# Dummy matmuls from a preamble constant, and tile 2's statistics placed behind tile 1's apply

## The chip, the cores and the metric

The kernel runs on one core of a Trainium2 chip. The metric is the device time of one execution in microseconds (us). The profiler's *span*, from the first to the last instruction of one execution, is 1.7 to 3.0 us shorter than the device time in the runs of these two kernels, 1.8 in the median. Engines: PE is TensorE, DVE is VectorE, ACT is ScalarE, POOL is GpSimd, SP is SyncE, which here only issues transfers.

## The reference

A layer norm of x (2048 rows of 640) feeds two branches. One is attention with 32 heads over the last 512 positions of a cache. The other is a gated feed-forward block, of whose start this study is about.

```python
xn = (x - mean(x)) / sqrt(var(x) + 1e-5)
s  = attention(xn, k_cache, v_cache, wq, wo)             # some 750 of the 920 us
g  = silu((silu(xn @ w_gate) * (xn @ w_up)) @ w_down)    # comes first
return x + s * g
```

## The kernel before

The first 13 us prepare four *tiles* of 128 rows of x, numbered 0 to 3. For each tile DVE makes the statistics in two halves and aggregates them, ACT takes the square root of the variance (Sqrt), DVE takes the reciprocal and applies it to x ("apply"), TensorE transposes the result by five matmuls against an identity matrix, and ACT copies the two parts out to `xnT`. The feed-forward matmuls of that tile follow. Before any of this, dummy matmuls on a zeroed tile keep TensorE busy, which is meant to have its clock at full rate when real work comes.

```python
zero_t = ffw.tile([P, 512], bf, name="zero_t")
nc.vector.memset(zero_t[:], 0.0)
...
load_x(0, (nc.scalar, nc.sync))
load_x(1, (nc.scalar,))
load_first(slice(0, 2), (nc.sync, nc.scalar))  # chunks 0, 1 of the gate and up weights
load_first(slice(2, NC))                       # chunks 2, 3, 4: gate, then up, both on SyncE
load_x(2, (nc.scalar,))
...
load_x(3)
...
keep_warm(9)        # nine dummy matmuls of 512 columns on zero_t
keep_warm(6, P)     # six of 128

def ln_stats(t, between=None):
    ...
    for g in range(ng):                 # two halves of the 640 columns
        nc.vector.bn_stats(stats[:, g, :], x_t[t][:, ...])
        if g == 0 and between:
            between()                   # apply of another tile stands between them
    nc.vector.bn_aggr(ln[b][0][:, ti, :], stats[:])

def ready(t):
    ...                                 # five transposes into tps[0], tps[1]
    for tp, cs in zip(tps, PARTS):
        if cs.stop == NC and 1 <= t < 3:
            ln_sqrt(t + 1)              # Sqrt of the next tile between the two copies
        ... nc.scalar.copy(xnT[:, cs, rows], part)

for t in range(4):
    ...
    for k, (f, s, cs) in enumerate(order):
        if k == len(order) * 7 // 10 and t < 3:
            if t < 2:
                ln_stats(t + 2, lambda: ln_apply(t + 1))
            else:
                ln_apply(t + 1)
            ready(t + 1)
            ...
        hidden_mm(first[f][s][:, rows], s, f, rows, cs)
```

For tile 0, `order` has 30 matmuls: twelve on weight chunks 0 and 1, nine on gate chunks 2 to 4, then (after tile 1's transposes) nine on up chunks 2 to 4. The second load of gate weights ("the late gate weights" below: 288 KB, chunks 2 to 4) is thus wanted just before tile 1's transposes.

The softmax here doesn't subtract the row's maximum and nothing guards it: scores larger than these inputs give would overflow.

## Time and profile before

| | before |
|---|---|
| median of the first 3 runs | 920.73 us (920.32 to 921.08) |
| profiled span | 919.1 us |
| TensorE busy | 912.6 us (99%) |
| tile 1's / 2's / 3's transposes start | 8.54 / 10.50 / 12.45 us |
| last group of matmuls starts | 915.06 us |

A line of the timeline gives start, duration, engine, source line, operation, output<-input, shape and count; in brackets stands the idle time of the engine before it and what ended that. A line of the waits gives who waited for whom, the total, the number and the longest.

### The profile page before, as it was taken

To read this page: it belongs to the slowest core of one execution; us is meant where nothing else is said; L and a number is where in the kernel's file an instruction comes from. 1 tells how busy PE (TensorE), PEld (TensorE's weight loads), DVE (VectorE), ACT (ScalarE), POOL (GpSimd) and SP (SyncE) were. 2 spreads that over 40 slices of the span, in tenths; PEclk is the share of its full clock that TensorE was granted. 3 is DMA by queue.
4 is the path that set the end of the run, shared out by engine and by line. 5 is a ranking of instruction groups with operands and counts; after the bars stand their busy time and mean duration, and the time that the engine had idled before them with its cause. 6 is when DMAs were issued, how large, how long until landed. Compare 5 with 4: busy or idle time off the path is not lost.

```text
span 919.1 us, 23152 instructions
## 1 busy us (share of the span) xinstructions
PE 912.6 (99%) x9898; PEld 548.9 (60%) x9920; DVE 601.7 (65%) x844; ACT 474.4 (52%) x840; POOL 85.3 (9%) x269
## 2 busy tenths in 40 slices
PE   9999999999999999999999999999999999999998
PEld 6444444465757575656565656666666666665665
DVE  6443321467777777777777777676867777777657
ACT  4222222556464656565656565655555555556471
POOL 0000000000000000000000000000000000001976
PEclk9999999999999999999999999999999999999999
DMA  9412430045352544263534343435243444343526
GB/s 302 76 34 65 90 84 1 1 75 113 54 113 49 112 51 107 54 109 54 109 58 109 57 109 52 109 54 107 56 85 76 88 79 78 87 71 102 118 61 166
DMA packets 248166, 77.53 MB, mean 84 GB/s; under 512 B 228992, under 2 KB 248064, under 8 KB 248064
## 3 DMA queue, kind: packets, MB, share of 16 engines
q1 hardware_dynamic: 245696, 73.39, 39.5%
q10 hardware_dynamic: 2368, 2.67, 0.9%
q8 instruction: 77, 1.26, 0.6%
q14 instruction: 25, 0.20, 0.1%
HBM read 38.93 MB, written 2.62 MB: 45 GB/s over the span
## 4 chain that ended last, share of the span: by engine, by line
PE 99%; DMA 1%; DVE 0%; ACTq 0%; issue 0%
PE mm L448 22%; PE sc L462 18%; PE mm L487 16%; PE sc L602 15%; PE sc L282 11%; PE mm L312 6%; PE sc L572 4%; PE sc L564 2%; PE mm L539 2%; PE mm L564 1%; DMA x_t<-in_A_x_dram 1%; PE gu L282 0%; PE mm L321 0%; PE sc L539 0%; PE sc L487 0%
## 5 line engine op out<-in xcount | busy, mean ns | idle before, releaser
L466 ACT ACTIVATE p_t<-sc 128x1024 bf16<-128x1024 f32 x254 | 253.0, 1023 | 120.3 <-PE sc L462 120.3
L453 DVE TENSOR_REDUCE qT<-mm 128x512 bf16<-128x1024 f32 x189 | 231.2, 1223 | 99.0 <-PE mm L448 96.5
L517 ACT ACTIVATE O_b<-mm,r 128x192 bf16<-128x192 f32 x486 | 165.0, 422 | 183.1 <-issue 136.6
L448 PE MATMUL mm<-xnT,wq_p 64*128 64x512 bf16 x1890 | 237.5, 376 | 0.0
L462 PE MATMUL sc<-qT,khat 64*128 64x512 bf16 x1524 | 198.0, 376 | 0.0
L487 PEld LDWEIGHTS <-p_t 64*128 64x128 bf16 x3584 | 159.0, 94 | 33.8
L487 PE MATMUL mm<-V_p,p_t 64*128 64x193 bf16 x3520 | 176.4, 243 | 0.0
L615 DVE TENSOR_TENSOR s_m<-s_m,sc 128x1024 f32<-128x1024 f32 x108 | 131.9, 1221 | 60.7 <-PE sc L602 52.3
L602 PE MATMUL sc<-wo_p,OT_b 64*128 64x512 bf16 x1296 | 168.9, 376 | 0.0
L448 PEld LDWEIGHTS <-wq_p 64*128 64x128 bf16 x1890 | 105.0, 94 | 98.9 <-issue 0.8
L462 PEld LDWEIGHTS <-khat 64*128 64x128 bf16 x1536 | 85.3, 94 | 80.4 <-DVE s_t L615 0.3
L602 PEld LDWEIGHTS <-OT_b 64*128 64x128 bf16 x1296 | 70.3, 94 | 44.1 <-issue 0.3
L615 DVE TENSOR_TENSOR s_t<-s_t,sc 128x512 f32<-128x512 f32 x108 | 74.2, 687 | 28.4 <-PE sc L572 26.6
L589 POOL MEMSET turn_t<- 128x1 f32 x220 | 21.6, 98 | 700.0 <-PE mm L487 506.0
L290 DVE TENSOR_TENSOR hT<-sc,sg 128x512 bf16<-128x512 f32 x46 | 31.7, 692 | 81.5 <-ACT sg L289 81.5
L289 ACT ACTIVATE sg<-sc 128x512 bf16<-128x512 f32 x46 | 27.3, 596 | 69.8 <-PE sc L282 66.7
L282 PE MATMUL sc<-xnT,wg_sb 128*128 128x512 bf16 (+1 forms) x255 | 60.1, 354 | 0.5
L282 PE MATMUL sc<-xnT,wu_sb 128*128 128x512 bf16 (+1 forms) x255 | 59.5, 355 | 0.2
L572 PE MATMUL sc<-OT_b,wo_p 64*128 64x512 bf16 (+1 forms) x345 | 50.3, 376 | 0.0
L312 PE MATMUL mm<-wd_sb,hT 128*128 128x512 bf16 x189 | 43.6, 379 | 0.2
L282 PEld LDWEIGHTS <-wu_sb 128*128 128x128 bf16 x285 | 27.1, 98 | 26.8 <-issue 0.3
L282 PEld LDWEIGHTS <-wg_sb 128*128 128x128 bf16 x285 | 27.2, 98 | 26.3
(83 smaller groups left out, 418.3 us busy)
## 6 DMA issues: line engine op xcount, KB each, us to landing
wo_p<-in_A_wo_dram SPq DMA_DIRECT2D x16, 480.0 KB, 4.7
K_p<-in_A_k_cache_dram SPq DMA_DIRECT2D x32, 192.0 KB, 4.4
V_p<-in_A_v_cache_dram SPq DMA_DIRECT2D x32, 192.0 KB, 3.3
wq_p<-in_A_wq_dram SPq DMA_DIRECT2D x64, 80.0 KB, 2.8
wq_p<-in_A_wq_dram SPq DMA_DIRECT2D x16, 160.0 KB, 3.0
x_t<-in_A_x_dram SPq DMA_DIRECT2D x13, 160.0 KB, 3.0
x_b<-in_A_x_dram SPq DMA_DIRECT2D x4, 512.0 KB, 6.1
OT_b<-O_b SPq DMA_TRANSPOSE x124, 2.8
```

What stands on the lines that cost most here:

```text
L282: nc.tensor.matmul(out, w_sb[:, c, f * P : (f + 1) * P], xnT[:, c, qc], start=(c == 0), stop=(c == NC - 1),)
L290: nc.vector.tensor_tensor(hTs[b][:, f, :], u, sg[:], ALU.mult)
L312: nc.tensor.matmul(dn, at, by, start=(f == 0), stop=(f == NF - 1))
L448: nc.tensor.matmul(q_ps[:, h, :], pairs[pr]["wq"][r, c, j * P : (j + 1) * P], xnT[r, c, b * 512 : (b + 1) * 512], start=(c == 0), stop=(c ...
L453: nc.vector.reduce_sum(qTs[i][:, j, :], q_ps[:, :, :].rearrange("p h n -> p n h"), axis=AX.X)
L462: nc.tensor.matmul(sc[:, h, :], khat[r, j, ks], qT[r, j, :], start=(j == 0), stop=(j == 2))
L466: nc.scalar.activation(p_t[:, :, :], sc[:, :, :], ACT.Exp, scale=scale)
L487: m = nc.tensor.matmul(acc[:, k, h * 256 : h * 256 + Dh + 1], Ps[i][kc][r, h, qt * P : (qt + 1) * P], V_p[r, kc, h, 0 : Dh + 1], start=(p ...
L517: nc.scalar.activation(O_b[:, qt, h, :], a_k[:, h, 0:Dh], ACT.Copy, scale=r[:, k, h, :])
L572: nc.tensor.matmul(ps.rearrange("p (t q) -> p t q", q=P), pairs[i // NB]["wo"][r, j, MC:D], OTs[i][:, :, :].rearrange("p (t j) q -> p j t ...
L602: m = nc.tensor.matmul(ps[:, k, :], OTs[i][r, 3 * (2 * half + k) + j, :], pairs[i // NB]["wo"][r, j, MAIN], start=(turn == 0 and j == 0), ...
L615: nc.vector.tensor_tensor(to, to, ps, ALU.add)
```

## The change

Its intent is to take two waits off TensorE at the start. The dummy matmuls read a constant that GpSimd writes before the engines start, so they need no memset by DVE. Tile 1's apply no longer stands between the halves of tile 2's statistics, whose data may not have landed; those statistics and tile 2's Sqrt come after tile 1's apply, transposes and copies. The diff, whole but for line numbers:

```diff
-        zero_t = ffw.tile([P, 512], bf, name="zero_t")
-        nc.vector.memset(zero_t[:], 0.0)
...
         def keep_warm(n, cols=512):
+            ones = [nc.const_aps.tensor(1.0, (P, k), bf) for k in (P, cols)]
             for _ in range(n):
-                nc.tensor.matmul(
-                    first[2][1][:, 0:cols], zero_t[:, 0:P], zero_t[:, 0:cols], start=True, stop=True
-                )
-
-        keep_warm(9)
+                nc.tensor.matmul(first[2][1][:, 0:cols], *ones, start=True, stop=True)
+
+        keep_warm(10)
         keep_warm(6, P)
...
-                if cs.stop == NC and 1 <= t < 3:
-                    ln_sqrt(t + 1)
+                if cs.stop == NC and t == 2:
+                    ln_sqrt(3)
...
-                    if t < 2:
-                        ln_stats(t + 2, lambda: ln_apply(t + 1))
+                    if t == 1:
+                        ln_stats(3, lambda: ln_apply(2))
                     else:
                         ln_apply(t + 1)
                     ready(t + 1)
-                    if t == 2:
+                    if t == 0:
+                        ln_stats(2)
+                        ln_sqrt(2)
+                    elif t == 2:
                         nc.scalar.activation(act_t[:], one_t[:], ACT.Silu)
```

## The prediction

> **What bounds the kernel now.** I read the page first, then the waits of TensorE over the whole span, then the timeline of the first 13 us engine by engine, because the diff touches only that stretch. The page says who owns the span: the matmul engine is busy from end to end, and the chain that ended last is nearly all its own instructions.
>
> ```profile
> span 919.1 us, 23152 instructions
> PE 912.6 (99%) x9898; PEld 548.9 (60%) x9920; DVE 601.7 (65%) x844; ACT 474.4 (52%) x840; POOL 85.3 (9%) x269
> PE 99%; DMA 1%; DVE 0%; ACTq 0%; issue 0%
> ```
>
> The reader is to see 919.1 - 912.6 = 6.5 us in which TensorE is not busy, and a DMA share of 1% of the chain: nothing else can be won by moving VectorE or ScalarE work. The view of TensorE's waits shows only two waits with a releaser in the whole run, both in the stretch that the diff touches:
>
> ```profile
> PE gu L230 <- DVE zero_t L176: 1.2, 1, 1.2
> PE tp L335 <- DVE xn L267: 0.5, 1, 0.5
> ```
>
> The first is the start (dummy matmuls wait for the zeroed tile), the second is the transposes of x tile 1 waiting for that tile's apply. So at most these 1.2 + 0.5 us are in play. VectorE's timeline gives the reason for the second:
>
> ```profile
> 6.27 0.21 DVE L246 BATCH_NORM_AGGREGATE mv<-stats 128x2 f32<-128x12 f32 x1
> 7.44 0.49 DVE L243 BATCH_NORM_STATS2 stats<-x_t 128x6 f32<-128x320 bf16 x1 [0.97 <-DMA x_t<-in_A_x_dram]
> 7.85 0.14 DVE L265 RECIPROCAL rstd<-rstd 128x1 f32<-128x1 f32 x1
> 8.03 0.45 DVE L267 TENSOR_SCALAR xn<-x_t,mv,rstd 128x640 bf16<-128x640 bf16 x1
> 8.39 0.48 DVE L243 BATCH_NORM_STATS2 stats<-x_t 128x6 f32<-128x320 bf16 x1
> 8.91 0.21 DVE L246 BATCH_NORM_AGGREGATE mv<-stats 128x2 f32<-128x12 f32 x1
> 9.04 0.44 DVE L243 BATCH_NORM_STATS2 stats<-x_t 128x6 f32<-128x320 bf16 x1
> ```
>
> At 7.44 VectorE takes the first half of tile 2's statistics, for which it idled 0.97 us until x tile 2 landed. Tile 1's reciprocal and apply stand behind it, though their input was there earlier, as ScalarE's timeline shows:
>
> ```profile
> 6.84 0.30 ACT L256 ACTIVATE rstd<-mv,eps_t 128x1 f32<-128x1 f32 x1
> 8.86 0.37 ACT L343 COPY xnT<-tp 128x256 bf16<-128x256 bf16 x1 [1.72 <-PE tp L335]
> 9.16 0.29 ACT L256 ACTIVATE rstd<-mv,eps_t 128x1 f32<-128x1 f32 x1
> 9.36 0.46 ACT L343 COPY xnT<-tp 128x384 bf16<-128x384 bf16 x1
> ```
>
> Tile 1's Sqrt is done at 6.84 + 0.30 = 7.14, and its reciprocal starts only at 7.85: 0.7 us lost to order. On TensorE:
>
> ```profile
> 7.85 0.22 PE L282 MATMUL gu<-xnT,wg_sb 128*128 128x128 bf16 x1
> 8.54 0.45 PE L335 MATMUL tp<-ident,xn 128*128 128x128 bf16 x5 [0.46 <-DVE xn L267]
> ```
>
> The listed idle time, 0.46 us, is counted from the modelled end of the matmul before. Counted in issue slots it is more: matmuls of 128 columns start 0.055 us apart here, so the slot after 7.85 is 7.91, and the transposes start at 8.54, **0.63 us late**.
>
> **What the Trainium skill says.** "TensorE: Matmul & The Clock Gate", in the table at its head, calls VectorE's and ScalarE's queues strict first-in-first-out; the trace agrees (the reciprocal above, held 0.7 us behind a wait that was not its own). The same page, Part 1, says the array runs at half rate until a free-running window of about 3.4 us has seen activity, with 427/107 ns between cold matmuls of 512/128 columns and 56 ns between warm ones of 128. The trace agrees on the spacing (dummies 0.43 us apart from 1.23 us on; real ones 0.11 apart until 6.94, 0.055 from 7.02); where the window falls in another run no trace of one execution shows. "ScalarE: Activation LUTs", Table sets, says that plain copies are in every table set, so copy-Sqrt-copy costs no reload; the trace agrees, with two loads of 1.28 us in this stretch, at 2.94 and 13.15, and none between. The change keeps the order of functions, so it adds none.
>
> **The change, part by part.**
>
> (a) Dummies. The 0.27 us memset at 0.90 goes; the matmuls read a constant that GpSimd wrote at 0.29, ahead of the start of all engines near 0.7 (the first queue entries of ScalarE and SyncE stand at 0.72). I take a start at 0.75 instead of 1.23. Before: 9 x 0.427 + 6 x 0.107 = 4.48, so to 5.71. After: 10 x 0.427 + 0.64 = 4.91, so to 5.66. The first real transposes start at 5.68 and need tile 0's apply, whose first part (two parts, 5.20 to 5.84) is there about 5.55. **Worth 0.0 to 0.05 us.** A side effect: activity starts 0.5 us earlier, so the clock may open earlier than 6.95. That would bring tile 1's Sqrt forward by perhaps 0.1 us, as tile 0's second copy waits for cold transposes.
>
> (b) Tile 1's apply no longer waits behind tile 2's statistics. Sqrt ends 7.14; reciprocal at 7.18 (0.04 later, as for tile 0: 4.96 to 5.00); apply 0.18 later, at 7.36, to 7.81; transposes ready 0.06 later (before: 8.48 to 8.54), at 7.87. TensorE's slot is 7.91. **The whole 0.63 us goes at this point.** What tile 1 needs next (copy, then matmuls) is a fixed distance behind the transposes: copy of part 0 starts 0.32 after them and takes 0.37, so 0.69; their first user is 0.79 after them. No new gap.
>
> (c) Tile 2's statistics now come after that apply, and I check whether they are in time. Apply to next statistics takes 0.36 (8.03 to 8.39): first half at 7.72, x tile 2 having landed by 7.44; second half some 0.42 later, at 8.14; aggregate 0.52 after that, 8.66 to 8.87. ScalarE: copies of tile 1 at 7.91 + 0.32 = 8.23 and about 8.57; the Sqrt follows the second copy's start by about 0.36 (tile 0: 6.48 to 6.84), so 8.93 to 9.22. Reciprocal 9.26, apply 9.44 to 9.89, transposes 9.95. TensorE arrives 1.96 after tile 1's transposes (8.54 to 10.50 before), at 9.87. So it waits about 0.08 us. **0.63 - 0.08 = 0.55 us is left.**
>
> (d) Tile 3 keeps its old order, Sqrt between the copies: relative to tile 2's transposes the apply ended in time before (11.61 + 0.45 = 12.06 for a start at 12.45, 0.39 to spare). After: transposes 9.95, copy 10.26, Sqrt 10.57 to 10.87, apply 11.1 to 11.55, slot 11.9. No wait.
>
> (e) From 8.54 on TensorE had no other wait that the profile names, to the end. The weights of later quarters are issued by SyncE, untouched by the change. So a shift at 10 us should arrive whole at 919 us. Sum: 0.55 us, rounded to **0.5 us**, about 0.06% of the time.
>
> **Rivals.** First, a new wait takes the place of the old: step (c) is tight, and if x tile 2 lands 0.5 us later than here, its statistics hold the apply of tile 2 instead. For it: DMA arrival sets that chain, and the landing at 7.44 is one sample. Against: there are 0.3 us of slack before 7.72. It would leave 0.1 to 0.5 us of gain. Second, the clock: if its window opens late (7.6 rather than 6.95), some 6 more of the first 21 matmuls run cold, 6 x 0.05 = 0.3 us, which the old wait hid and the new order doesn't. It leaves a gain of 0.25; an early opening makes it 0.65 or so. Third, the constant may be one column read 512 times; if such reads ran at half rate, the ten dummies would end near 10 us and put the first transposes back by 4 us, to 925 us. Nothing in this profile shows such a read; I give it 2%. Fourth, nothing seen: three runs of the old kernel spread over 0.76 us (920.32 to 921.08), more than the gain.
>
> **Range and chances.** 920.73 - 0.5 = 920.2 us. The rivals give gains of 0.1 to 0.7, and a median of three runs carries perhaps 0.3 us of scatter by the spread above; together 919.6 to 920.8. Two per cent would be 18 us, ten times what these two waits hold altogether, so the verdict is "same" but for an accident.
>
> **What would show it.** Right: no named wait of TensorE for an apply above 0.2 us; tile 1's transposes near 7.9, tile 2's near 9.95, tile 3's near 11.9; two copies of tile 1 with nothing between and Sqrt near 8.93; dummies starting near 0.75 at 0.43 us spacing; the matmul of 512 columns that began at 14.97 beginning near 14.4. Wrong: dummies further apart than 0.43 us; tile 2's first statistics later than 8 us with a DMA named; a gap of TensorE elsewhere that gives the shift back before the end.

## The result

The changed kernel's median is 920.65 us (920.08 to 921.6, six runs), against 920.81 us (920.32 to 921.24, six runs) of the kernel before. A ratio here is the mean time of one kernel's fast runs over that of the other's in the same rounds, so not quite the ratio of the medians. It is 1.0000, with a 95% interval of 0.9987 to 1.0013: the same time. Half a microsecond was forecast, and the times show none. (The median lies inside the range that the prediction gave, 919.6 to 920.8, but that of the kernel before misses its upper end by only 0.01, so this lends the forecast no support.)

The one profile, however, shows nearly what was forecast. Page of the changed kernel (span; busy time, share and instructions; shares of the chain that ended last):

```profile
span 918.5 us, 23175 instructions
PE 914.0 (100%) x9921; PEld 551.1 (60%) x9921; DVE 601.5 (65%) x843; ACT 473.9 (52%) x840; POOL 85.2 (9%) x269
PE 99%; DVE 0%; ACT 0%; issue 0%
```

The span is 0.6 us shorter, and the transfer of x is gone from the chain. TensorE's waits in the changed kernel are down to one line, its start:

```profile
PE gu L229 <- PEq L842: 0.8, 1, 0.8
```

VectorE's timeline of the changed kernel:

```profile
6.17 0.21 DVE L243 BATCH_NORM_AGGREGATE mv<-stats 128x2 f32<-128x12 f32 x1
7.09 0.16 DVE L262 RECIPROCAL rstd<-rstd 128x1 f32<-128x1 f32 x1 [0.72 <-ACT rstd L253]
7.29 0.45 DVE L264 TENSOR_SCALAR xn<-x_t,mv,rstd 128x640 bf16<-128x640 bf16 x1
7.66 0.88 DVE L240 BATCH_NORM_STATS2 stats<-x_t 128x6 f32<-128x320 bf16 x2
8.57 0.21 DVE L243 BATCH_NORM_AGGREGATE mv<-stats 128x2 f32<-128x12 f32 x1
```

ScalarE's:

```profile
6.76 0.30 ACT L253 ACTIVATE rstd<-mv,eps_t 128x1 f32<-128x1 f32 x1
8.12 0.75 ACT L340 COPY xnT<-tp 128x256 bf16<-128x256 bf16 x2 [1.06 <-PE tp L332]
8.81 0.29 ACT L253 ACTIVATE rstd<-mv,eps_t 128x1 f32<-128x1 f32 x1
```

TensorE's, with tile 1's, 2's and 3's transposes:

```profile
7.11 0.22 PE L279 MATMUL gu<-xnT,wu_sb 128*128 128x128 bf16 x1
7.29 0.28 PE L279 MATMUL sc<-xnT,wg_sb 128*128 128x128 bf16 x2
...
7.75 0.22 PE L279 MATMUL gu<-xnT,wg_sb 128*128 128x128 bf16 x1
7.80 0.45 PE L332 MATMUL tp<-ident,xn 128*128 128x128 bf16 x5
8.18 0.28 PE L279 MATMUL sc<-xnT,wu_sb 128*128 128x128 bf16 x2
...
9.87 0.44 PE L332 MATMUL tp<-ident,xn 128*128 128x128 bf16 x5
...
11.82 0.44 PE L332 MATMUL tp<-ident,xn 128*128 128x128 bf16 x5
```

The reciprocal now follows tile 1's Sqrt at once (7.06 to 7.09), the two copies stand together, and the transposes of tiles 1, 2 and 3 start 0.74, 0.63 and 0.63 us earlier than before. Two short waits stand here that the view of waits does not list, since the modelled end of one matmul covers the gap: the matmuls at 7.29 and 8.18 had slots near 7.16 and 8.08. They come back below. The last group of matmuls, from the end of the two timelines, first of the kernel before and then of the changed one:

```profile
915.06 0.49 PE L564 MATMUL sc<-wo_p,OT_b 128*128 128x256 bf16 x3
```

```profile
914.43 0.49 PE L564 MATMUL sc<-wo_p,OT_b 128*128 128x256 bf16 x3
```

That is again 0.63 us. The question for the experiments is why a shift that is so clean between two profiles is not in the mean of the times.

### The profile page after: what moved, and what is told of

Same layout as the page of the kernel before. It is cut to its first block, busy times and chain, and to the rows that moved or that the text cites. A ratio compares the mean times of both kernels' runs of the same rounds, so it can differ in the third digit from the quotient of the medians.

```text
span 918.5 us, 23175 instructions
## 1 busy us (share of the span) xinstructions
PE 914.0 (100%) x9921; PEld 551.1 (60%) x9921; DVE 601.5 (65%) x843; ACT 473.9 (52%) x840; POOL 85.2 (9%) x269
## 4 chain that ended last, share of the span: by engine, by line
PE 99%; DVE 0%; ACT 0%; issue 0%
PE mm L448 22%; PE sc L462 18%; PE mm L487 16%; PE sc L602 15%; PE sc L279 11%; PE mm L309 6%; PE sc L572 4%; PE sc L564 2%; PE mm L539 2%; PE mm L564 1%; PE gu L229 1%; PE gu L279 0%; PE mm L318 0%; PE sc L539 0%; PE sc L487 0%; PE mm L462 0%
```

## The experiments

Two theories. **Steady shift**: every execution gains about 0.6 us, and scatter hid it. **Exposed start**: the gain depends on when transfers land, the first profile was an unusual one, and in most executions another wait takes the place of the one removed. Sixteen kernels ran, all timed in five rounds beside the kernel before. In all, the unedited kernel before ran 63 times.

"The clock opened" means that TensorE's granted clock went from half to full. Landings below were read from the trace: the time at which a transfer's semaphore took its last increment, in us from the start of the span.

### The two kernels again, and each half of the change alone

`a1_after_again` is the changed kernel, unedited.

> The changed kernel once more, unedited, to average out the scatter. Steady-shift theory (every execution is shorter by the 0.6 us seen between the two profiles, and scatter of 0.8 to 1.5 us hid it in medians of six): mean of the timed runs 0.4 to 0.8 us below the kernel before of the same rounds; in the profile the transposes of x tile 1 start at 7.8 +- 0.1 and the long matmuls of the fourth hidden slice near 14.35. Exposed-start theory (the new order lays bare a clock window or a landing that the old wait hid, so the gain shrinks in many executions): mean gain under 0.3 us, and a profile with a later start, tile 1's transposes at 8.1 or later in some.

Measured: mean 921.5 us over five runs, ratio to before 1.0002. Tile 1's transposes start at 8.08, and TensorE waits 0.2 us for the late gate weights. The last group starts at 914.65, 0.41 earlier than in the first profile of before, and yet the span is 919.6. Its end shows why. Final stores, with KB and us to landing, in this run:

```profile
out_dram<-x_b ACTq DMA_DIRECT2D x1, 96.0 KB, 2.6
out_dram<-x_b SPq DMA_DIRECT2D x1, 64.0 KB, 2.5
```

and in the first profile of the changed kernel:

```profile
out_dram<-x_b ACTq DMA_DIRECT2D x1, 96.0 KB, 1.8
out_dram<-x_b SPq DMA_DIRECT2D x1, 64.0 KB, 1.6
```

The last stores took 0.8 to 0.9 us longer to land: more than the whole gain, and nothing that the change touches.

`a2_before_again` is the kernel before, unedited, as a null.

> The kernel before, unedited, as a null: both theories say 0.0 +- 0.3 us against itself. What it measures is the scatter of a difference of two equal kernels, and a second profile: if the transposes of x tile 1 start at 8.54 +- 0.05 again, the start is steady; if they move by 0.3 us or more with the landing of x tile 2, the scatter comes from that landing.

Measured: ratio 0.9994 against itself, so a difference of 0.06% is what two equal kernels show. Tile 1's transposes at 8.54 once more, x tile 2 landing at 7.42 once more; but here the late gate weights land at 7.65, after x, and cost a wait of 0.3 us that the wait for x then hides.

`a3_dummies_only` has only the first two parts of the diff (constant, ten dummies), with the old order.

> Only the dummy matmuls changed (constant, ten of them), old order of the statistics. Both theories: dummies from 0.76 us, but tile 1's transposes still wait for the landing of x tile 2, 8.4 to 8.6 us, and the end moves by 0.0 to 0.1 us. If it gains 0.3 or more, the start of the dummies was worth more than the prediction's 0.05.

Measured: mean 921.5 us, ratio 1.0004. The dummies start at 0.76 us. Tile 1's transposes start at 8.14, outside the expected 8.4 to 8.6: x tile 2 landed at 7.02, not 7.42. They follow that landing by 1.12 us as in the kernel before, so the dummies gave nothing; the landing moved by itself. That was the first sign that the landing at 7.42 is not a constant.

`a4_order_only` has only the new order, with the zeroed tile and nine dummies.

> Only the new order of tile 2's statistics, with the old zeroed tile and nine dummies. Steady-shift theory: tile 1's transposes at 7.9, tile 2's at 9.9 to 9.95, and 0.5 to 0.6 us less than before in the profile and in the mean of the timed runs. Exposed-start theory: the first real matmuls run cold to about 7, the gain is 0.2 to 0.4 us.

Measured: mean 920.6 us, ratio 0.9992. Transposes at 7.54, 9.78 and 11.73, last group at 914.34, span 918.4, the earliest of all. The clock opened at 4.79 here, and x tile 2 landed at 6.73 and the late gate weights at 6.89, both the earliest of all profiles with these loads, so this early end is not the order's alone. With a3 it says that the dummies add nothing that these profiles show, and that what there is of a gain comes from the order.

### What tile 1 waits for

`b1_no_landing`: old order, but the first half of tile 2's statistics reads x tile 1. The statistics are wrong, though the output still passed the comparison.

```diff
-                nc.vector.bn_stats(stats[:, g, :], x_t[t][:, ...])
+                src = x_t[1] if t == 2 and g == 0 else x_t[t]
+                nc.vector.bn_stats(stats[:, g, :], src[:, ...])
```

> Old order and old dummies, but the first half of tile 2's statistics reads x tile 1, which has landed (its numbers are then wrong on purpose). Nothing else moves. If the landing of x tile 2 ahead of tile 1's apply is the cause: tile 1's transposes at 7.6 to 8.1 us as in the new order, instead of 8.1 to 8.54, the last matmul group earlier by the same. If the order on VectorE itself costs (0.4 us of statistics ahead of the apply), 8.0 or later even so.

Measured: the reciprocal of tile 1 starts at 7.01, so the landing of x tile 2 (7.82 here) was what held it. But the transposes start only at 8.69, because TensorE waits 1.0 us for the late gate weights, which land at 8.13. The expectation of 7.6 to 8.1 failed, and showed the second gate: with x out of the way, weights are next. Mean 921.05, ratio 0.9999.

`b2_late_x2_old_order`: the kernel before with the loads of x tiles 2 and 3 exchanged; `b3_late_x2_new_order`: the changed kernel with the same edit.

```diff
-        load_x(2, (nc.scalar,))
+        load_x(3, (nc.scalar,))
...
-        load_x(3)
+        load_x(2)
```

> Old order, with the loads of x tiles 2 and 3 exchanged, so that tile 2 lands later, near 8.6 us by tile 3's landing in the profiles so far. Landing theory: tile 1's transposes follow it by 1.1 us, to 9.5 to 9.8, tile 3's to 13.4 to 13.8, and the end moves by the same 1.1 us: about 921.8 in the timed mean. Rival (time is made up later): the end moves by less than half of it.

> New order, with the same exchange. Tile 1's transposes stay at 7.6 to 8.1; tile 2's wait for landing, statistics, Sqrt and apply, about 2.2 us after the landing, 10.6 to 10.9; tile 3's at 12.6 to 12.9. So 0.7 to 0.9 us ahead of the old order with the same exchange, in the profile and at the end; the timed means differ by 0.3 to 1.3 with the scatter seen so far. Rival (exposed start gives the gain back): under 0.4.

Measured, old order: x tile 2 lands at 9.19, tile 1's transposes follow 1.12 later at 10.31, and the mean is 922.8 (ratio 1.0018; 922.4 without the slowest run). New order: x tile 2 lands at 9.86, and the mean is 921.9 (ratio 1.0008). In the old order the landing came 1.9 us later than in the mean of the 14 profiles that leave these loads alone (7.30), and the mean time 1.7 us later (1.3 without the slowest run), so the rival, less than half of it, fails. With the landing made late the order is worth 0.9 us in the times (95% interval about 0.0 to 1.9; 0.8 without each one's slowest run), as expected, although the landing itself came later than assumed and tile 1's transposes stood at 9.22, behind gate weights that landed at 8.66. No other pair differs by as much. The old-order run also shows a cost that I had not thought of. Busy time in the clock's windows of the old-order run (columns: us, then busy time and instruction count by engine, granted clock, share of the transfer engines, GB/s):

```profile
7.65:11.07 3.42, 1.44 (x23) 1.27 (x24) 1.79 (x6) 0.44 (x2) 0.00 (x0) 1.00 1.10 333
11.07:14.48 3.41, 3.41 (x36) 3.41 (x34) 1.47 (x6) 1.19 (x5) 0.00 (x0) 0.50 1.10 334
```

TensorE was busy for 1.44 of 3.42 us, and then its clock was at half for one window. This profile's span is 922.5, while the other four runs of the kernel had 920.3 to 921.1.

`b4_sqrt_between`: the changed kernel, but tile 2's Sqrt stays between the copies of tile 1.

```diff
-                if cs.stop == NC and t == 2:
-                    ln_sqrt(3)
+                if cs.stop == NC and 1 <= t < 3:
+                    ln_sqrt(t + 1)
...
                     else:
                         ln_apply(t + 1)
-                    ready(t + 1)
                     if t == 0:
                         ln_stats(2)
-                        ln_sqrt(2)
-                    elif t == 2:
+                    ready(t + 1)
+                    if t == 2:
```

> The changed kernel, but with tile 2's Sqrt still between the two copies of tile 1. My working says that the second copy then waits for the aggregate of tile 2 (about 8.8 us), ends near 9.5, and is wanted near 9.2: tile 2's transposes at 10.1 to 10.2 in place of 9.8 to 10.0, so 0.2 to 0.3 us of the gain lost. If moving the Sqrt was worth nothing, tile 2's transposes stand 1.95 to 2.0 us after tile 1's.

ScalarE's timeline of that run:

```profile
8.23 0.37 ACT L340 COPY xnT<-tp 128x256 bf16<-128x256 bf16 x1 [1.06 <-PE tp L332]
8.92 0.29 ACT L253 ACTIVATE rstd<-mv,eps_t 128x1 f32<-128x1 f32 x1 [0.32 <-DVE mv L243]
9.12 0.46 ACT L340 COPY xnT<-tp 128x384 bf16<-128x384 bf16 x1
```

The copy does wait, 0.32 us, for tile 2's aggregate, as worked out; the next matmuls of TensorE start at 9.63 in place of a slot at 9.37, and tile 2's transposes start at 10.13, 2.22 us after tile 1's. Without a wait they follow by 1.96. So in this profile the placing of the Sqrt costs 0.26 us, inside the 0.2 to 0.3 expected. (The changed kernel has 1.99 to 2.24 in its own four profiles, with `a4_order_only`, but there the excess has another cause, told below the table.) In the times it is lost: the mean, 920.5, is even below the others.

### Weights, and repeats

`c1_x2_behind_wg_new` (new order) and `c4_x2_behind_wg_old` (old order) load x tile 2 on SyncE's queue behind the late gate weights.

```diff
-        load_first(slice(2, NC))
-        load_x(2, (nc.scalar,))
+        nc.sync.dma_start(out=wg_sb[:, 2:NC, 0:FQ], in_=...)
+        load_x(2)
+        nc.sync.dma_start(out=wu_sb[:, 2:NC, 0:FQ], in_=...)
```

> New order, with the load of x tile 2 moved behind the second gate-weight load on SyncE's queue, so that these weights, which the first matmuls want at 7.2 us, have less beside them. If the weights' landing is the floor of the new order: they land by 7.1, no wait for them, tile 1's transposes at 7.6 to 7.9 whatever else; tile 2's at 9.8 to 10.2; a span of 918.3 to 918.7 with a short tail. If the queue's order does not matter, weights wait 0.2 to 0.3 us as in most profiles so far.

> Old order with the same moved load as the first of these runs. x tile 2 lands at 7.3 to 7.7, tile 1's transposes 1.10 us after it, 8.4 to 8.8; so 0.5 to 1.0 us behind the new order with this load order, at tile 3 0.3 to 0.8. If it equals the new order within 0.2, tile 2's landing is not what decides.

Measured, new order: the weights land at 7.04 and are not waited for; transposes at 7.90 and 10.10; span 918.9, a little above the expected range; mean 921.3, ratio 1.0001. Old order: x tile 2 lands at 8.08, later than expected, and tile 1's transposes follow at 9.20. At tile 3 the old order is 1.07 us behind (13.12 to 12.05). As a version to keep, the first of the two gains nothing that the times show.

`c2_after_third` and `c3_before_third` are the two kernels unedited.

> The changed kernel a third time. Landing theory: tile 1's transposes at the later of 7.8 us and 0.55 us after the landing of the second gate weights; last matmul group 902.6 us after tile 3's transposes; mean gain over all timed runs 0.2 to 0.4 us. Prediction as it stood: 0.55 in the mean.

> The kernel before a third time. Landing theory: tile 1's transposes 1.10 us after the landing of x tile 2 (or 0.55 after the weights, if that is later), tile 3's 3.91 us after tile 1's, the last matmul group 902.6 after that. Against itself 0.0 +- 0.4 us.

Measured: the pair has the roles reversed. The kernel before has x tile 2 landing at 6.92, transposes at 8.04, a last group at 914.67 and a span of 918.7. In the changed kernel TensorE's waits and tile 1's transposes read

```profile
PE sc L279 <- DMA wg_sb<-in_B_w_gate_dram: 0.9, 1, 0.9
...
8.62 0.44 PE L332 MATMUL tp<-ident,xn 128*128 128x128 bf16 x5
```

because the late gate weights landed at 8.06; the span is 919.3. Ratios 0.9998 for the changed kernel, 0.9993 for the old kernel against itself.

### The late gate weights taken out of the way

`d1_weights_there_new` and `d2_weights_there_old`: tile 0's gate matmuls of chunks 2 to 4 were to read weight chunks that have landed (wrong on purpose; the output still passed the comparison).

```diff
+                wc = c - 2 if s == 0 and c >= 2 and qc == slice(0, P) else c
-                    out, w_sb[:, c, f * P : (f + 1) * P], xnT[:, c, qc],
+                    out, w_sb[:, wc, f * P : (f + 1) * P], xnT[:, c, qc],
```

> New order; tile 0's gate matmuls of chunks 2 to 4 read chunks 0, 1 and 0, which have landed (results wrong on purpose). If the landing of the second gate weights is the floor: no wait for weights, and tile 1's transposes at 7.5 to 7.9 us, about 0.7 after the start of tile 1's reciprocal, however late those weights land. If something else holds TensorE there: 8.0 or later.

> Old order with the same edit. Tile 1's transposes 1.12 us after the landing of x tile 2, as in all old-order profiles so far (7.8 to 8.5 for the landings seen); so 0.3 to 0.6 us behind the new order with the edit, where the unedited pair differs by 0.3 at tile 1 and 0.2 at tile 3. The timed means may show 0.2 to 0.5; their scatter is 0.6 a run.

Measured: the edit was off by one. Chunk 4 read chunk 2, which belongs to the late load, so three of the nine matmuls still waited, and the expectation's "chunks 0, 1 and 0" was not what ran. It is an accidental half-dose: in the new order the weights landed at 7.65 and the transposes started at 7.87, 0.22 us after them in place of 0.56. In the old order the transposes started at 9.00, 1.12 us after x tile 2. Ratios 0.9999 and 1.0001.

`d3_weights_there_new` and `d4_weights_there_old` repeat it with `c % 2`.

> New order; tile 0's gate matmuls of chunks 2, 3 and 4 read chunks 0, 1 and 0 (results wrong on purpose). If the late weights are the floor: no wait for weights, tile 1's transposes 0.73 to 0.77 us after the start of tile 1's reciprocal (7.5 to 7.9), also where those weights land after 7.3. If another thing holds TensorE: 8.0 or later.

> Old order with the same edit: no wait for weights, tile 1's transposes 1.12 us after the landing of x tile 2, wherever that falls. So the difference of the two orders is here the whole wait for x tile 2, 0.2 to 0.9 us for the landings seen, 0.45 in the middle.

Waits of TensorE, tile 1's reciprocal and tile 1's transposes in the new order:

```profile
PE sc L280 <- DMA wu_sb<-in_B_w_up_dram: 0.5, 1, 0.5
PE tp L333 <- DVE xn L264: 0.5, 1, 0.5
...
6.97 0.16 DVE L262 RECIPROCAL rstd<-rstd 128x1 f32<-128x1 f32 x1 [0.50 <-ACT rstd L253]
...
7.67 0.45 PE L333 MATMUL tp<-ident,xn 128*128 128x128 bf16 x5
```

Tile 2's first statistics and tile 1's transposes in the old order:

```profile
7.51 0.49 DVE L243 BATCH_NORM_STATS2 stats<-x_t 128x6 f32<-128x320 bf16 x1 [1.09 <-DMA x_t<-in_A_x_dram]
...
8.61 0.45 PE L336 MATMUL tp<-ident,xn 128*128 128x128 bf16 x5 [0.98 <-DVE xn L267]
```

In the new order the late gate weights landed at 7.80 and no longer matter: the transposes start at 7.67, 0.70 us after the reciprocal. (0.73 to 0.77 was expected.) With d1 this shows that these weights are the floor of the new order at tile 1 when they land late: taken out of the way, tile 1's transposes no longer follow them. Yet the 0.94 us between the two runs at tile 1 is only 0.21 us at tile 3 (12.32 and 12.53): the next load, of the up weights, landed at 8.63 and was waited for by 0.5 us; part of the 0.94 is also that x tile 2 landed 0.33 later in the old order's run. Ratios 0.9993 and 1.0002 (the old order's mean has one run of 924.33 in it).

### All profiles together

| run | order | x tile 2 lands | late gate weights land | up weights land | tile 1's transposes | tile 2's | tile 3's | last group | span |
|---|---|---|---|---|---|---|---|---|---|
| before | old | 7.42 | 7.06 | 8.04 | 8.54 | 10.50 | 12.45 | 915.06 | 919.1 |
| a2 | old | 7.42 | 7.65 | 8.35 | 8.54 | 10.50 | 12.46 | 915.07 | 919.3 |
| a3 (dummies) | old | 7.02 | 7.27 | 8.12 | 8.14 | 10.11 | 12.06 | 914.67 | 918.7 |
| c3 | old | 6.92 | 7.38 | 8.38 | 8.04 | 10.11 | 12.06 | 914.67 | 918.7 |
| after | new | 7.07 | 7.24 | 8.13 | 7.80 | 9.87 | 11.82 | 914.43 | 918.5 |
| a1 | new | 7.27 | 7.52 | 8.22 | 8.08 | 10.07 | 12.04 | 914.65 | 919.6 |
| a4 (order) | new | 6.73 | 6.89 | 8.04 | 7.54 | 9.78 | 11.73 | 914.34 | 918.4 |
| c2 | new | 7.63 | 8.06 | 8.95 | 8.62 | 10.68 | 12.63 | 915.24 | 919.3 |

"Up weights" are those of chunks 2 to 4, for the nine matmuls after tile 1's transposes. Four rules can be read off.

- In the old order tile 1's transposes stand 1.12 us after the landing of x tile 2, each time.
- In the new order they stand 0.56 us after the landing of the late gate weights, in three of four (in a4 they come later than that, when the apply is done; in "after" the apply would allow the same 7.80).
- From tile 3's transposes to the last group it is 902.61 us, in every row.
- The matmuls on the up weights start 0.04 to 0.05 us after they land, if tile 1's transposes are through by then (8.18 after 8.13 in "after", 8.09 after 8.04 in a4, 8.99 after 8.95 in c2, 8.42 after 8.38 in c3), and tile 2's transposes stand 1.73 or 1.74 us after that landing in these four, as in b1, c1, d1 and d3; in the other profiles, but for b2, b3 and b4, they follow tile 1's by 1.96 to 1.99.

So at tile 1 the order is worth 1.12 - 0.56 = 0.56 us, less the time by which the weights land after x. In the first profile of before the weights landed 0.36 us *before* x. In all 13 other profiles that left the order of these loads alone (the other seven rows, with b1 and b4 and d1 to d4) they landed 0.13 to 0.64 us *after* it, 0.28 in the mean. That leaves some 0.28 us (the four rows of each order differ there by 0.31 in the mean). Of the two theories it is the exposed start that holds.

At tile 3 less is left: the four rows of the new order have their third transposes at 12.06 in the mean, the four of the old order at 12.26, a gain of 0.20 us; the rest goes to the up weights, the floor at tile 2 in three of the four new rows and in one of the old. The times of these two kernels cannot show this. Over all runs the kernel before has a mean of 921.04 us (63 runs, standard deviation 0.60), the changed kernel 921.11 us (16 runs, 0.60), so the gain is -0.08 with a 95% interval of -0.40 to 0.25. With a4's runs added as well (21) it is 0.05, -0.24 to 0.33. A gain of 0.2 lies inside, the forecast (920.73 - 920.2 = 0.53) outside both. The spans of the same runs say the same, -0.05 with -0.38 to 0.28 (57 and 16 runs that list one). Pooled after the fact with the edited kernels that keep these loads and one of the two orders (a4, b4, d1 and d3 as new, a3, d2 and d4 as old; 36 and 79 runs) the gain is 0.24, 0.01 to 0.46. That fits 0.2, but the edits differ and the pool was not planned.

## Why the prediction was wrong

**What held.** TensorE is the bound, and nothing but its waits in the first 13 us was in play. The reciprocal of tile 1 was held by x tile 2's landing and only by queue order (b1: without the landing it starts at 7.01). The dummies were worth nothing (a3), as worked out at 0.0 to 0.05, and those on the constant start 0.43 us apart (1.13, 1.56, 1.99), so the third rival is out. The second did not occur: the clock had opened by 6.96 in every profile. Tile 2's transposes were put at 9.95 and came at 9.87, tile 3's at 11.9 and came at 11.82, and the long matmuls put near 14.4 began at 14.34. So near a match in the first profile was partly luck: its late gate weights landed at 7.24, among the earliest. Step (e), that the shift arrives whole at the end, holds to 0.01 us.

**The step that failed** is (b): "**The whole 0.63 us goes at this point.**", with its "No new gap." Its term of 0.63 us measured some 0.28 us in the usual execution, because of something that the table shows. I looked for what tile 1's transposes wait for on DVE's and ACT's side and never asked when the weights of the nine matmuls ahead of them land. In the one profile I had, they had landed at 7.06, in time: the matmuls at 7.35 and 7.41 show no gap. That was the unusual thing in it. In the 14 profiles that leave these loads alone they landed at 6.89 to 8.13, 7.53 in the mean, and by the second rule they are the floor of the new order in most; b1, c2 and d3 show it with and without. The landing of x tile 2 at 7.42 was an ordinary one (6.73 to 7.88, mean 7.30). The prediction did call that landing "one sample", but its first rival used this only for a later landing of x in the new order, and of the weights' landing it took none. Some of the old wait for x was thus only standing in front of a wait for weights.

**The smaller step** is (c), a loss of 0.08 us at tile 2 because its apply comes late. In the table the way from tile 1's to tile 3's transposes is 3.91, 3.92, 3.92 and 4.02 us in the old order and 4.02, 3.96, 4.19 and 4.01 in the new: 0.10 lost in the mean. The size is right, the cause mostly not: by the fourth rule the loss in "after", a4 and c2 is a wait for the up weights, which (c) does not have, and only a1's 0.03 is left to the late apply. What (c) says of the Sqrt held: left between the copies it costs 0.26 (b4).

**The scatter.** The prediction gave a median of three runs "perhaps 0.3 us" of scatter. One run scatters by 0.60 us (standard deviation); by my estimate from that, a median of six carries about 0.3 and the difference of two such about 0.4, nearly the gain forecast. The kernel before against itself differed by 0.06 and 0.07%. Part of it is shown: the start moves by 0.4 us in the old order and 0.9 in the new, and the final stores once took 0.8 us longer to land. In the other rows the span ends 4.04 to 4.20 us after the start of the last group (a1: 4.90). But timed runs had spans to 920.5 and one of 921.5, above those of the profiles of the two kernels, and those left no trace; what made them long stays open. So does the part outside the span, which is 1.7 us in some runs and 3.0 in one (921.99 us with a span of 919.0).

**Left open.** One timed run of the kernel before (923.42 us, span 921.5) and one of d4 (924.33, span 922.4), both in the old order, list a granted clock of 0.998, the figure of the profile of b2 in which the clock fell to half for a window. No run in the new order lists it. It may be that a long wait at the start sometimes costs the old order time in this way, but without a trace of such a run it is not shown, and two in so many runs hardly move a mean.

## What to carry to other kernels

A wait in one profile is one draw where a transfer ends it: before giving its removal a value, ask when every *other* input of the next instructions landed in that same profile, and how these landings stand to each other in a second and third execution. When a wait of half a microsecond is taken away amid transfers that run at full rate, the next landing is often right behind it, here twice: gate weights, then up weights. A wait of 0.1 or 0.2 us may not be listed at all; compare the starts of matmuls with their slots. And a gain below the scatter of one run is better measured as an interval inside several traces (here from one marked instruction to the last) than as a time.

## What the Trainium skill lacked or had wrong

- "TensorE: Matmul & The Clock Gate", Part 1, gives "≥1 idle window (~3.4µs)" for the fall to half clock, and its table of practical rules warns of idle gaps above some 3 us. In b2 the clock fell after a window in which TensorE was busy for 1.44 of 3.42 us, with no single wait above 1.74 us. In b3 a window with 1.74 us of 3.41 busy left it up. So in these two runs the limit lay between 42 and 51% busy (as the profile counts it), not at an idle window. The page also tells of a kernel whose many short idles let the clock swing, but gives no share.
- The same page says that one busy window opens the clock. With dummy matmuls back to back from 1.23 or 0.76 us, the profiles show it open at the end of the first window where they had filled 81% of it or more (c4: from 1.23, open at 3.99; c1: from 0.76, open at 3.56) and only one window later where they had filled 68% or less (before: 6.96; after: 6.49). The opening falls anywhere between 3.56 and 6.96 us, which agrees with the page's free-running window; the half-rate stretch of b2 lasted 3.41 us, the length that it gives for a window. What it lacks is the share: here between 68 and 81%.
- No page that I read says how far the landing of one load moves between executions when many are in flight. Here x tile 2 (160 KB, issued at 2.42 us) landed between 6.73 and 7.88, the late gate weights (288 KB, issued at 2.24) between 6.89 and 8.13, in the 14 profiles that leave these loads alone, at transfer engines that were busy throughout (share 1.10 in the windows of b2 above).
